# A mixer kernel whose last first-layer product is formed by seven block products for eight

## The chip, the cores and the metric

The kernel runs on one core of a Trainium2 chip. The metric is the device time of one execution in microseconds, as the median of several runs. TensorE (PE) multiplies matrices into PSUM, which has eight banks of 512 fp32 columns by 128 partitions; VectorE (DVE), ScalarE (ACT) and GpSimd (POOL) work element by element, the first two also on PSUM; SyncE (SP) issues nearly all transfers, in the order of its queue.

## What is computed

Attention with a few sink positions and a window, then a mixing of low rank along the sequence, then an FFN with a residual:

```python
B, H, S, D = 4, 8, 768, 64
scores = where(is_sink | in_window, q @ k.T / 8, -1e9)   # 4 sinks, window 128
a = softmax(scores) @ v                                  # per batch and head
x = a.transpose(0, 2, 1, 3).reshape(B, S, 512)
u = x + (x.T @ U @ V).T                                  # rank 32, along S
out = u + maximum(u @ w_ch1, 0) @ w_ch2                  # 512 -> 2048 -> 512
```

The inputs are 64-bit floats. The kernel narrows them to fp32, and keeps fp32 accuracy on PE by splitting an operand into a rounded high part and a rest, `hi + lo`: a product is then three matmuls, `hi*lo + lo*hi + hi*hi`.

## The kernel before

Lines are those of the kernel before. All work is written down as steps with an engine, a duration, what they read and write, and a rank (`Plan.add`, `Plan.any`, L232 on). `Plan.order` then plays the steps through with list scheduling: `forward` starts, in the order of time, the best-ranked step that is ready on each engine; `backward` derives new ranks from the latest times; eleven rounds run and the best planned end is kept. The steps are then issued in the order of their planned starts. So the order of every queue follows from the planned costs, `mm`, `dve`, `act`, `gps` (L420 on), and from the dependencies. Some steps may go to any of two or three engines (`copy` and `tt`), and the plan chooses. A buffer of a ring (`Ring`, `Box`) is waited for until the steps on its former content are done. PSUM banks are a free ring of eight.

**Batch 0 and batch 1** attend heads in pairs (`attend_pair`): scores of two heads (L652), then per block `soften`, a masked row minimum on DVE (L704) and an exponential with row sum on ACT (L707). `normalise` forms the inverse of the sums for each head (L715, reciprocal on DVE at L718) and scales. `transposes` turns the weights on PE (L745); for these batches the first part is masked by a product with a triangle on DVE as it leaves PSUM (L754), the second is copied and masked by a selection on POOL (L770). L675 multiplies by the values. **Batches 2 and 3** attend head by head (`attend`) with hi/lo operands (L695, L696, L793), and mask both parts on POOL (L767, L770). `mix_start`, `mix_half` and `mix_end` do the low-rank mixing (L889 to L982; L974 is its last product) and leave `uh` and `ul`, the transposed FFN input in high and low parts, by chunk of 384 rows.

**The FFN** (`ffn(b, c, ...)`) handles one chunk of 384 rows against 16 blocks of 128 features. `l1` is the first product of a block: 4 contraction slices x 3 matmuls of 384 columns (L1006, L1007, L1008) into one bank, then relu to `hh` on ACT or DVE (L1014, L1015) and the rest `hl` on DVE (L1017). `l2` is the second: for each of three row blocks three matmuls of 512 columns (L1027) into one of three banks held for the whole chunk. `l1(i)` is written ahead of `l2(i-1)`. For batch 0 the weights are narrowed on the way (`narrow`, L99 to L107, on DVE, ACT and POOL), and blocks other than 0 and 8 are stored as 1 MB units in `wd`, to be fetched again by the later batches through four tiles; blocks 0 and 8 stay resident in two more. At the end of a chunk DVE adds the residual (L1053) in `big` buffers, a ring of four which the narrowing of weights also uses, and SP stores the rows. L482 is where all of SP's transfers are issued.

Attention of batch b+1 is planned beside the FFN of batch b. Before the plan's first step there is a preamble with eight "spin" matmuls of zeros (L1320), the first loads, and the making of masks.

Of the kernel before, what the change touches and what calls it, by code (L numbers as in the profile page):

```python
# [9 lines left out]
F32 = mybir.dt.float32  # L10
# [11 lines left out]
P = 128  # L22
# [14 lines left out]
HALF = NBLK * SW  # L37
NEG = 8.0e9
# [3 lines left out]
NSPIN = 8  # L42
ROUNDS = 10
SLACK = 0.0344
SAME = 0.0842
PRICE = {"DVE": 3.0, "ACT": 1.5, "POOL": 1.5}
NBANK = 8
NRES = 2
# [14 lines left out]
LEAD = 30.0  # L63
BESIDE = ((6, 2.5), (0, 2.5), (0, 2.5))
# [10 lines left out]
def f32(ap):  # L75
    return ap.bitcast(F32)
# [163 lines left out]
class Plan:  # L240
# [35 lines left out]
    def order(self):  # L276
# [11 lines left out]
        for s, p in zip(self.steps, best[1]):  # L288
            s.prio = p
        self.forward()  # L290
        return sorted(self.steps, key=lambda s: (s.start, s.n))

    def backward(self):
# [20 lines left out]
        while done < len(self.steps):  # L314
# [5 lines left out]
            for p, whole in before[s]:  # L320
                p.left -= 1
                sync = self.SYNC[p.eng] if p.eng != e else (0.0 if e == "PE" else SAME)
                p.ready_b = max(p.ready_b, s.back + p.lat + sync + (1.95 if p.eng == "SP" else 0.0) if whole else s.back - p.dur)
# [6 lines left out]
    def forward(self):  # L330
# [37 lines left out]
        while done < len(self.steps):  # L368
            turn = sorted((max(avail[e], min(at(s, e) for s in lst)), e) for e, lst in ready.items() if lst)
            pick = None  # L370
# [19 lines left out]
            if e == "SP":  # L390
                dma = max(dma, t + s.dur + 0.65) + s.lat
                end = dma + 1.3
# [47 lines left out]
class Fast:  # L440
# [38 lines left out]
    def put(self, box, pair, nbytes, prio, r=(), part=None, rows=P):  # L479
# [3 lines left out]
        self.plan.add("SP", 0.5 if rows == P else 0.65, fn, r=r, w=((box, part),) if box else (), lat=nbytes / 330e3, prio=prio)  # L483

    def narrow(self, src, n, prio, dst=()):

        raw, A, S_ = self.raw(), self.nr(), self.nr()
        if len(self.early) > 0:
            self.early.pop(0)
        else:  # L490
# [143 lines left out]
    def attend_pair(self, b, pr, half, t0, qk, v, xT):  # L634
# [5 lines left out]
        sms = [self.ms(), self.ms()]  # L640
        for u in range(NBLK):
# [12 lines left out]
            add("PE", 0.105 + wd / 600.0, mms, r=[qr, kr] + [(p, u) for p in ps], w=sts, prio=t0, after=self.gate)  # L654
            for st, p, sm in zip(sts, ps, sms):
                self.soften(st, p, sm, u, lo, wd, qb, t0)
# [25 lines left out]
    def scores(self, half, t0, qs, kh, kl, qbase=0, kbase=0):  # L682
        nc, add = self.nc, self.plan.add
        p, sm = self.p(), self.ms()
        for u in range(NBLK):
# [12 lines left out]
            self.soften(st, p, sm, u, lo, wd, qb, t0)  # L698
        return p, sm

    def soften(self, st, p, sm, u, lo, wd, qb, t0):
# [4 lines left out]
            -0.125, 3.0e38, ALU.add, ALU.min, sm()[:, u:u + 1]), r=(st,), w=((p, u), (sm, u)), prio=t0)  # L706
        add("ACT", act(wd) + 0.22, lambda: nc.scalar.activation(  # L707
            p()[:, u, NS + lo:], p()[:, u, NS + lo:], AF.Exp, bias=sm()[:, u:u + 1], scale=-1.0,
# [694 lines left out]
```

## Time and profile before

| | us |
|---|---|
| median of 3 runs | 753.34 |
| lowest and highest | 753.15, 753.82 |
| span of the profiled execution, first to last instruction | 750.5 |

The profiled execution has a span only, which leaves out what lies around the instructions; the median is 2.84 us above it. The profile's page gives the busy time of each engine and how the span is spent, and the trace behind it can be asked for groups of instructions by line, for waits, for the chain of work that ended last, for a stretch in order of time, and for busy time by stage. Matmuls are pipelined: their durations overlap, and their spacing is read from their starts.

### The profile page before, as it was taken

The numbers are of one execution on the slowest core, as the hardware profiler recorded it, in microseconds if no ns is written. First come the engines' busy times: TensorE is split into PE (matmuls) and PEld (weight loads), VectorE is DVE, ScalarE is ACT, GpSimd is POOL, SyncE is SP. The second block draws the span as 40 slices with busy tenths as digits, with TensorE's granted clock in tenths as the row PEclk, the third lists the DMA queues.
The fourth block names the chain that finished last, engine by engine and source line by source line (L and its number), as shares of the span: only waits on it lengthen the run. The fifth ranks groups of instructions, "written<-read, shape, count | busy, mean of one in ns | idle before, by whom it ended". The sixth has DMA issues, their size and how long they took to land.

```text
span 750.5 us, 11587 instructions
## 1 busy us (share of the span) xinstructions
PE 727.3 (97%) x4012; PEld 629.2 (84%) x4012; DVE 454.3 (61%) x1168; ACT 341.4 (45%) x977; POOL 194.0 (26%) x316
## 2 busy tenths in 40 slices
PE   7989999999998999999999999999999999999997
PEld 5557777777787999999899899999999989889895
DVE  7999889798999577667751287675653131112111
ACT  6986475775874445555541164564441111111110
POOL 4652030421521263263510043544401000000000
PEclk9999999999999999999999999999999999999999
DMA  7466758755795378563575468760276536524752
GB/s 261 150 197 226 261 182 302 258 184 205 240 296 223 124 244 278 177 209 117 167 241 183 153 194 256 231 211 1 71 263 227 169 135 237 199 76 138 267 176 96
DMA packets 43780, 146.84 MB, mean 196 GB/s; under 512 B 5440, under 2 KB 12224, under 8 KB 34240
## 3 DMA queue, kind: packets, MB, share of 16 engines
q1 hardware_dynamic: 43424, 145.62, 57.7%
q8 instruction: 33, 0.54, 0.3%
q10 hardware_dynamic: 288, 0.39, 0.2%
q14 instruction: 35, 0.29, 0.1%
HBM read 116.37 MB, written 29.62 MB: 195 GB/s over the span
## 4 chain that ended last, share of the span: by engine, by line
PE 84%; DVE 11%; ACT 1%; issue 1%; DMA 1%; POOL 0%; SPq 0%; DVEq 0%; ACTq 0%
PE bank L1027 33%; PE bank L1006 12%; PE bank L1007 11%; PE bank L1008 11%; PE bank L793 3%; PE bank L745 2%; PE bank L652 2%; PE bank L675 2%; DVE nr L104 2%; PE bank L695 2%; PE bank L696 2%; DVE w L474 1%; DVE bank L106 1%; PE bank L906 1%; DVE p L704 1%
## 5 line engine op out<-in xcount | busy, mean ns | idle before, releaser
L1027 PE MATMUL bank<-w,hh 128*128 128x512 f32 x768 | 246.2, 402 | 1.2 <-ACT hh L1014 0.6
L1017 DVE SCALAR_TENSOR_TENSOR hl<-bank,hh 128x384 fp32r<-128x384 f32 x128 | 70.9, 554 | 186.9 <-ACT hh L1014 186.1
L1006 PE MATMUL bank<-ul,w 128*128 128x384 f32 x512 | 178.5, 349 | 0.8 <-ACT w L467 0.7
L1007 PE MATMUL bank<-uh,w 128*128 128x384 f32 x512 | 174.0, 340 | 1.8 <-DVE w L474 1.8
L1008 PE MATMUL bank<-uh,w 128*128 128x384 f32 x512 | 173.1, 338 | 0.0
L1014 ACT ACTIVATE hh<-bank 128x384 fp32r<-128x384 f32 x121 | 59.3, 490 | 236.6 <-PE bank L1008 235.9
L1027 PEld LDWEIGHTS bank<-w,hh 128*128 128x128 f32 x768 | 139.6, 189 | 24.5 <-issue 1.4
L1027 PE MATMUL bank<-w,hl 128*128 128x512 f32 x384 | 151.8, 395 | 2.3 <-DVE hl L1017 2.3
L1006 PEld LDWEIGHTS bank<-ul,w 128*128 128x128 f32 x512 | 96.3, 188 | 12.1 <-issue 3.4
L1007 PEld LDWEIGHTS bank<-uh,w 128*128 128x128 f32 x512 | 96.4, 188 | 8.6 <-DVE w L474 3.7
L1008 PEld LDWEIGHTS bank<-uh,w 128*128 128x128 f32 x512 | 96.2, 188 | 0.0
L1027 PEld LDWEIGHTS bank<-w,hl 128*128 128x128 f32 x384 | 72.2, 188 | 20.8 <-DVE hl L1017 3.6
L707 ACT ACTIVATE p<-p,ms 128x132 f32<-128x132 f32 (+1 forms) x144 | 69.9, 486 | 33.4 <-DVE ms L704 32.9
L704 DVE CUSTOM_DVE_ANT_0 p<-bank,mask 128x132 f32<-128x132 f32 (+1 forms) x144 | 54.3, 401 | 13.3 <-PE bank L696 10.8
L476 POOL TENSOR_TENSOR p<-p 128x256 f32<-128x256 f32 (+1 forms) x26 | 21.7, 836 | 131.0 <-ACT p L707 130.3
L476 POOL TENSOR_TENSOR ul<-xT,uh 128x384 fp32r<-128x384 f32 x14 | 14.4, 1050 | 146.0 <-ACT uh L467 146.0
L467 ACT COPY tb<-bank 64x384 f32<-64x384 f32 x31 | 14.7, 474 | 40.0 <-PE bank L793 40.0
L729 POOL TENSOR_TENSOR p<-p,r 128x396 f32<-128x396 f32 x27 | 24.2, 898 | 32.4 <-DVE r L718 26.0
L474 DVE TENSOR_TENSOR xT<-bank,tb 64x384 f32<-64x384 f32 x32 | 17.5, 548 | 23.1 <-ACT tb L467 22.8
L770 POOL TENSOR_SCALAR_AFFINE_SELECT oph<-oph 128x384 fp32r<-128x384 f32 (+1 forms) x48 | 27.4, 572 | 12.8 <-ACT oph L467 10.2
L745 PE MATMUL bank<-ident,p 128*128 128x128 f32 x144 | 24.9, 278 | 3.4 <-POOL p L729 2.2
L770 POOL TENSOR_SCALAR_AFFINE_SELECT opl<-opl 128x384 fp32r<-128x384 f32 (+1 forms) x48 | 26.1, 544 | 7.4 <-ACT opl L467 4.1
(187 smaller groups left out, 1137.7 us busy)
## 6 DMA issues: line engine op xcount, KB each, us to landing
w<-wd SPq DMA_DIRECT2D x60, 1024.0 KB, 4.9
big<-in_w_dram SPq DMA_DIRECT2D x32, 512.0 KB, 4.2
wd<-w SPq DMA_DIRECT2D x14, 1024.0 KB, 4.4
big<-xd SPq DMA_DIRECT2D x33, 256.0 KB, 3.2
qkraw<-in_k_dram SPq DMA_DIRECT2D x32, 198.0 KB, 5.3
qkraw<-in_q_dram SPq DMA_DIRECT2D x32, 192.0 KB, 4.0
out_dram<-big SPq DMA_DIRECT2D x24, 256.0 KB, 2.2
v_raw<-in_v_dram SPq DMA_DIRECT2D x16, 192.0 KB, 3.2
```

Of the source, the lines that this page charges most:

```text
L474: ways = {"DVE": (dve(n), lambda: nc.vector.tensor_tensor(dst(), a(), b(), op), pool)}
L476: ways["POOL"] = (gps(n), lambda: nc.gpsimd.tensor_tensor(dst(), a(), b(), op), True)
L704: add("DVE", dve(wd), lambda: nc.vector.tensor_tensor_reduce(p()[:, u, NS + lo:], st()[:, :wd], self.mask[:, min(qb, 2), lo:], -0.125, 3.0 ...
L707: add("ACT", act(wd) + 0.22, lambda: nc.scalar.activation(p()[:, u, NS + lo:], p()[:, u, NS + lo:], AF.Exp, bias=sm()[:, u:u + 1], scale=-1.0,
L745: nc.tensor.transpose(tr()[:, u * P:(u + 1) * P], p()[:, u, SW + NS:], self.ident)
L770: add("POOL", 0.126 + CH * 0.914e-3, lambda t=t: nc.gpsimd.affine_select(as_(t()[:, :, 1, :]), f32(t()[:, :, 1, :]), [[0, NBLK], [1, P]], ...
L1006: nc.tensor.matmul(ph()[:, :CH], wh, ul()[:, d, :], start=d == 0, stop=False)
L1007: nc.tensor.matmul(ph()[:, :CH], wl, uh()[:, d, :], start=False, stop=False)
L1008: nc.tensor.matmul(ph()[:, :CH], wh, uh()[:, d, :], start=False, stop=d == NC - 1)
L1014: self.plan.any({"ACT": (act(CH), lambda: nc.scalar.activation(hh(), ph()[:, :CH], AF.Relu)), "DVE": (dve(CH), lambda: nc.vector.tensor_sc ...
L1017: add("DVE", dve(CH), lambda: nc.vector.scalar_tensor_tensor(hl(), ph()[:, :CH], 0.0, f32(hh()), ALU.max, ALU.subtract), r=(ph, hh), w=(hl ...
L1027: nc.tensor.matmul(acc[k](), a()[:, sl], w()[:, m, :], start=not begin and i == 0 and j == 0, stop=i == n - 1 and j == 2)
```

## The change

1. **The last batch's FFN** is one pass over both chunks (`ffn_last`), by pairs of blocks. With the contraction in two halves, the features of a pair as two halves and the two chunks as two halves, a pair's first product is a 2x2 by 2x2 block product. It is formed by seven block products (Strassen's scheme, in the variant with shared sums) and not eight. Each product is 2 slices x 3 matmuls of 384 columns. Sums are gathered in two banks, x and y, with copies to SBUF between. The second product goes on as before, into six banks. `seven` prepares seven operands from batch 3's FFN input, in hi/lo parts, in buffers that attention has left; `sums` prepares four sums of the weight blocks of each pair, during the FFN of batch 1 (second chunk) and batch 2 (first chunk), and stores them as 1 MB units in `sd`. All 16 weight units are in `wd` now, and the six weight tiles are reused by pairs.
2. **Softmax inverses** of a pair of heads are formed by one reciprocal (`inverse`), and in batch 1 both masks are made on POOL (`late`).
3. **PE early:** 12 spin matmuls instead of 8, and 30 matmuls of zeros planned with the lowest rank.
4. **The planner** has other cost figures for matmuls, scores and transfers, knows when the first weights land (`EARLY`), and tries ranks shaken at random (three seeds), kept only where the planned end falls.
5. The kernel is built with a smaller scratch area for dynamic transfers.

```diff
+SUMS = {(1, 1): (0, 1, 2, 3), (2, 0): (7, 6, 5, 4)}
-NSPIN = 8
+NSPIN = 12
+NIDLE = 30
+SEEDS = (300012, 300023, 300026,)
+RATE = 360e3
+EARLY = (0.55, 1.5, 2.5, 3.8)
...
 def order(self):
+        for seed in SEEDS:
+            best = self.shaken(seed, best)
...
 def mm(n, k=1):
-    return k * max(n + (44 if n > CH else 34), 262) / 2400.0
+    return k * max(n * 1.085 + 6, 262) / 2400.0
...
 def put(...):
-        ... lat=nbytes / 330e3, prio=prio)
+        ... lat=nbytes / RATE, prio=prio)
...
 def attend_pair(...):
-        sms = [self.ms(), self.ms()]
+        sm = self.ms()
-            add("PE", 0.105 + wd / 600.0, mms, ...)
+            add("PE", 0.165 + wd / 600.0, mms, ...)
+        r = self.inverse(sm, 2 * NBLK, t0)
         for i in range(2):
-            self.normalise(b, 2 * pr + i, half, t0 + i, ps[i], sms[i], self.sinks[b])
-            ts += self.transposes(half, t0 + i, ps[i], True, self.opl if i else self.oph)
+            self.normalise(b, 2 * pr + i, half, t0 + i, ps[i], r, i * NBLK, self.sinks[b])
+            ts += self.transposes(half, t0 + i, ps[i], True, self.opl if i else self.oph, b > 0)
...
 def transposes(...):
-        if whole:
+        if whole and not late:
             ... product with the triangle on DVE ...
         else:
-            self.copy(CH, top, v3, psum=True, ...)
+            self.copy(CH, lambda: as_(top()), v3, psum=True, ...)
         for t in res:
-            if not whole:
+            if late:
                 add("POOL", 0.126 + nu * P * 0.914e-3, ... affine_select ...)
...
+    def seven(self, b, t0):
+        b11, b12, b21, b22 = src(0, 0), src(0, 1), src(1, 0), src(1, 1)
+        for i, x, y, ... in ((0, b12, b11, ...), (1, b22, t[0], ...), (2, b22, b12, ...), (3, b21, t[1], ...)):
+            for dd in range(2):
+                self.tt(CH, t[i](dd), x(dd), y(dd), ALU.subtract, ...)
+        for i, x, ... in ((0, b11), (1, b21), (2, b22), (3, t[3]), (4, t[0]), (5, t[1]), (6, t[2])):
+            for dd in range(2):
+                self.copy(CH, hi(dd), x(dd), ...)
+                self.tt(CH, lo(dd), x(dd), f32(hi(dd)), ALU.subtract, ...)
...
+    def sums(self, j, ws, prio):
+        for i, w in enumerate(ws):
+            self.tt(DM, fa()[:, i * DM:(i + 1) * DM], f32(w()[:, 0]), f32(w()[:, 1]), ALU.add, ...)
+        for i, o, x, y, op, r in ((0, s1, a21, a22, ALU.add, []), (1, s2, s1, a11, ALU.subtract, [(t, 0)]),
+                                  (2, s3, a11, a21, ALU.subtract, []), (3, s4, a12, s2, ALU.subtract, [(t, 1)])):
+            self.tt(K2, o, x, y, op, ...)
+        self.copy(2 * DM, hi, ft, ...)
+        self.tt(2 * DM, lo, ft, f32(hi()), ALU.subtract, ...)
+        for i, (x, y) in enumerate(((a, hi), (t, lo))):
+            self.put(sd, ..., 1 << 19, prio, r=(x,), part=i)
...
+    def ffn_last(self, b, prio):
+        order = late[2:] + [None] + late[:2] + [None]
+        def unit(key, dram):
+            i, old, f = slots.pop(0)
+            if f is None or f != key:
+                w = Box(lambda i=i: self.wtiles[i], (old,))
+                self.put(w, ..., 1 << 20, prio, r=(dram,))
+            slots.append((i, w, None))
+        def l1(n):
+            j = NPF - 1 - n
+            w1, w2, wt = unit(2 * j, self.wd[2 * j]), unit(2 * j + 1, self.wd[2 * j + 1]), unit(None, self.sd[j])
+            p1 = product(x, r12, w1, half(w1, 0), 0, True, self.line)
+            self.line = (p1,)
+            product(y, r2, w1, half(w1, 1), 1, True)
+            snap(sa, ta, 0)
+            plus(t11, tb, 1, sa, ta, 0)
+            relu(0, 0, t11, (tb, 1), False)
+            product(x, r12, wt, comb(1), 5)
+            product(y, r2, wt, comb(2), 6, True)
+            snap(sb, ta, 1)
+            product(x, r12, wt, comb(0), 4)
+            snap(sc, tb, 0)
+            plus(t22, tc, 1, sc, tb, 0)
+            relu(1, 1, t22, (tc, 1), False)
+            product(x, r12, wt, comb(3), 2)
+            relu(0, 1, r12, x, True)
+            product(y, r2, w2, half(w2, 1), 3)
+            plus(t21, tc, 0, sb, ta, 1)
+            relu(1, 0, t21, (tc, 0), False)
+        for n in range(NPF + 1):
+            if n < NPF:
+                l1(n)
+            if n == 0:
+                ... start six sums with vst and T ...
+            else:
+                l2(n - 1)
+        for k in range(NB):
+            o, ud = self.big(), self.xd[b][k]
+            ... load the residual, add on DVE, store ...
...
 def ffn(...):
+            if f // 2 in SUMS.get((b, c), ()) and f ^ 1 in fs[:i]:
+                self.sums(f // 2, pair, prio)
...
 def run(self):
+        for _ in range(NIDLE):
+            box = self.bank()
+            self.plan.add("PE", 0.22, lambda box=box: nc.tensor.matmul(box()[:, :P], zero, zero, ...),
+                          w=(box,), prio=1e6)
+            elif b == B - 1:
+                self.ffn_last(b, 70.0 + 80.0 * NCHUNK * b)
+                for f in range(NF) if b == 1 else ():
+                    if f not in STREAMED:
+                        self.put(self.wd[f], ..., 1 << 20, 200.0, r=(self.w[f],))
```

In this listing the arguments are shortened. `snap` is a copy from x, `plus` an addition of y to a copy, `relu` two operations.

## Rows read from the trace of the kernel before

**Rows 1.** The page, part 1: busy us, share of the span, instructions.
```profile
PE 727.3 (97%) x4012; PEld 629.2 (84%) x4012; DVE 454.3 (61%) x1168; ACT 341.4 (45%) x977; POOL 194.0 (26%) x316
```

**Rows 2.** Busy time by stage: stage and length, then engines, granted clock, DMA share, GB/s.
```profile
0.00:10.00 10.00, 7.70 (x40) 7.00 (x40) 5.45 (x32) 4.07 (x13) 2.39 (x14) 1.00 0.73 257
10.00:240.00 230.00, 215.23 (x1230) 163.57 (x1227) 213.15 (x577) 159.36 (x458) 74.15 (x105) 1.00 0.67 227
240.00:608.30 368.30, 367.77 (x2071) 335.85 (x2070) 212.95 (x523) 162.29 (x477) 117.48 (x197) 1.00 0.56 182
608.30:745.00 136.70, 136.62 (x678) 122.82 (x677) 22.07 (x40) 15.70 (x32) 0.00 (x0) 1.00 0.51 176
```

**Rows 3.** Order of time, 734 to 739 us, PE: start, duration, line, operation.
```profile
734.73 0.34 PE L1006 MATMUL bank<-ul,w 128*128 128x384 f32 x1
...
736.14 0.34 PE L1008 MATMUL bank<-uh,w 128*128 128x384 f32 x1
...
736.32 0.64 PE L1027 MATMUL bank<-w,hh 128*128 128x512 f32 x2
...
738.42 0.34 PE L1006 MATMUL bank<-ul,w 128*128 128x384 f32 x1
```

**Rows 4.** The chain that ended last, two neighbouring pieces: start, duration, what.
```profile
685.76 2.11 PE bank L1027 x9
689.99 2.11 PE bank L1027 x9
```

**Rows 5.** Order of time, same stretch, ACT and DVE; in brackets idle time before.
```profile
736.51 0.49 ACT L1014 ACTIVATE hh<-bank 128x384 fp32r<-128x384 f32 x1 [3.73 <-PE bank L1008]
...
737.04 0.56 DVE L1017 SCALAR_TENSOR_TENSOR hl<-bank,hh 128x384 fp32r<-128x384 f32 x1 [3.67 <-ACT hh L1014]
```

**Rows 6.** DMA issues: names, count, KB each, median us to landing; last the final additions.
```profile
w<-wd SPq DMA_DIRECT2D x60, 1024.0 KB, 4.9
...
big<-xd SPq DMA_DIRECT2D x33, 256.0 KB, 3.2
...
out_dram<-big SPq DMA_DIRECT2D x24, 256.0 KB, 2.2
```

**Rows 7.** Batch 3's last mixing product (order of time), and busy time by stage after.
```profile
564.29 0.34 PE L974 MATMUL bank<-vst,t 128*128 128x384 f32 x1
...
570.00:600.00 30.00, 30.00 (x151) 27.06 (x150) 3.90 (x7) 3.54 (x8) 0.00 (x0) 1.00 0.58 205
```

**Rows 8.** Groups by shape, DVE, 240 to 608.3 us: busy, mean ns, idle before.
```profile
L474 DVE TENSOR_TENSOR xhl<-first1q,xhl 128x512 fp32r<-128x512 f32 x5 | 3.5, 693 | 4.5 <-PE bank L929 4.0 <-ACT xhl L467 0.6
```

**Rows 9.** Order of time at 233 us.
```profile
228.21 4.04 DVE L982 TENSOR_TENSOR xT<-xT,bank 128x384 f32<-128x384 f32 x8
...
233.38 0.50 PE L1027 MATMUL bank<-w,hl 128*128 128x512 f32 x1 [2.11 <-DVE hl L1017]
```

**Rows 10.** Groups by shape, DVE, 0 to 240 us.
```profile
L718 DVE RECIPROCAL r<-r 128x3 f32<-128x3 f32 x32 | 4.5, 160 | 0.7 <-ACT r L715 0.7
L754 DVE TENSOR_TENSOR opl<-bank,tri 128x384 f32<-128x384 f32 x8 | 4.4, 550 | 0.5 <-ACT opl L467 0.4
...
L754 DVE TENSOR_TENSOR opl<-bank,tri 128x256 f32<-128x256 f32 x8 | 3.3, 416 | 0.2 <-PE bank L745 0.2
```

**Rows 11.** POOL's selections (f32: batches 0, 1), a DVE addition's mean, one addition at 15 us.
```profile
L770 POOL TENSOR_SCALAR_AFFINE_SELECT opl<-opl 128x384 fp32r<-128x384 f32 x32 | 16.6, 519 | 0.5
...
L770 POOL TENSOR_SCALAR_AFFINE_SELECT opl<-opl 128x384 f32<-128x384 f32 x16 | 9.5, 593 | 6.9 <-ACT opl L467 4.1 <-DVE opl L468 2.8
...
L474 DVE TENSOR_TENSOR p<-p 128x256 f32<-128x256 f32 x3 | 2.5, 826 | 0.0
...
15.53 0.39 DVE L474 TENSOR_TENSOR qkraw<-qkraw 128x256 f32<-128x256 f32 x1
```

**Rows 12.** Order of time, 6 to 13 us: three groups of score matmuls.
```profile
6.05 2.54 PE L652 MATMUL bank<-first0k,first0q 64*128 64x132 f32 x12 [1.45 <-DVE m_ck L161]
...
8.35 1.98 PE L652 MATMUL bank<-first1k,first1q 64*128 64x132 f32 x12
...
11.40 1.37 PE L652 MATMUL bank<-kh,qs 64*128 64x132 f32 x12 [1.06 <-DVE ms L704]
```

More of the change, by code (lines that the diff above doesn't have):

```diff
@@ L1 @@
+import random
 import struct
@@ L287, in order, with put_back, shaken @@
                 self.backward()
-        for s, p in zip(self.steps, best[1]):
-            s.prio = p
+        for seed in SEEDS:
+            best = self.shaken(seed, best)
+        self.put_back(best[1])
         self.forward()
         return sorted(self.steps, key=lambda s: (s.start, s.n))
+    def put_back(self, prios):
+        for s, p in zip(self.steps, prios):
+            s.prio = p
+    def shaken(self, seed, best):
+        rnd = random.Random(seed)
+        by, t, width = rnd.choice((0.3, 1.0, 3.0, 8.0)), rnd.uniform(-20.0, 260.0), rnd.choice((20.0, 60.0, 300.0))
+        if rnd.random() < 0.2:
+            t += 280.0
+        self.put_back(best[1])
+        self.forward()
+        for s in self.steps:
+            g = rnd.gauss(0.0, by)
+            if t <= s.start < t + width:
+                s.prio += g
+        for _ in range(TURNS):
+            try:
+                self.forward()
+            except ValueError:
+                break
+            if self.span < best[0] - 1e-6:
+                best = self.span, [s.prio for s in self.steps]
+            self.backward()
+        return best
     def backward(self):
@@ L322, in backward @@
                 sync = self.SYNC[p.eng] if p.eng != e else (0.0 if e == "PE" else SAME)
[L323 removed]
+                p.ready_b = max(p.ready_b, s.back + max(p.lat, 0.0) + sync + (1.95 if p.eng == "SP" else 0.0) if whole else s.back - p.dur)
                 if not p.left:
@@ L389, in forward @@
             end = t + s.dur + s.lat
-            if e == "SP":
+            if e == "SP" and s.lat < 0.0:
+                end = -s.lat
+                dma = max(dma, end - 1.3)
+            elif e == "SP":
                 dma = max(dma, t + s.dur + 0.65) + s.lat
@@ L482, in fn @@
             self.nc.sync.dma_start(d, s)
-        self.plan.add("SP", 0.5 if rows == P else 0.65, fn, r=r, w=((box, part),) if box else (), lat=nbytes / 330e3, prio=prio)
+        self.plan.add("SP", 0.5 if rows == P else 0.65, fn, r=r, w=((box, part),) if box else (), lat=nbytes / RATE, prio=prio)
     def narrow(self, src, n, prio, dst=()):
@@ L489, in narrow @@
             self.early.pop(0)
+            self.plan.add("SP", 0.0, lambda: None, w=(raw,), lat=-EARLY[NBIG - 1 - len(self.early)], prio=-1e6)
         else:
@@ L736, in normalise, with transposes @@
                       r=(p,), w=((psink, (half, h)),), prio=t0)
-    def transposes(self, half, t0, p, whole, own=None):
+    def transposes(self, half, t0, p, whole, own=None, late=True):
         nc, add = self.nc, self.plan.add
@@ L761, in transposes @@
         else:
-            self.copy(CH, top, v3, psum=True, r=(tr,), w=((res[0], 1),), prio=t0)
+            self.copy(CH, lambda: as_(top()), v3, psum=True, r=(tr,), w=((res[0], 1),), prio=t0)
+        if not whole:
             self.tt(CH, lambda: res[1]()[:, :, 1, :], v3, lambda: f32(top()), ALU.subtract, pool=False,
```

188 lines of the change are left out of this document (167 added, 21 removed).

## Prediction

> **What bounds the kernel now.** First the page's table of engines: TensorE (PE) is busy for 97% of the span [rows 1], so only a change to PE's work, or to what PE waits for, can move the end. Then busy time by stage [rows 2]. Three stages have to be told apart. From 240 to 608 us (FFN of batches 1 and 2, attention of 2 and 3 laid between) PE lacks 0.5 us of 368.3; from 608.3 to 745 us (FFN of batch 3) it lacks 0.1 us of 136.7, with VectorE (DVE) busy for 22 us and ScalarE (ACT) for 16. There a matmul taken away is time gained, and a microsecond taken from another engine is nothing. From 10 to 240 us PE lacks 14.8 us of 230 while DVE is busy for 213: DVE, which attends batches 0 and 1 and narrows the weights, sets the pace, and PE's idle time is what could be won. Since a busy PE need not be PE at its peak, 14.8 is a floor for that; 15 to 20 is my estimate. Before 10 us PE lacks 2.3 us.
>
> For PE's price I read starts, not durations: a matmul "lasts" 0.34 us, but from 734.73 to 736.14 us eight of the 384-wide ones start, 0.176 us each, and from 736.32 to 738.42 us nine of the 512-wide ones, 0.233 each [rows 3]. The chain of waits repeats every 4.23 us per feature block of `ffn` (689.99 less 685.76) [rows 4]: 12 of the first kind, 9 of the second. Nothing else fits in, and 2 x 16 x 4.23 = 135.4 us plus six starting matmuls is the whole stage.
>
> **The change, part by part.**
>
> (a) *Seven products for eight.* The first product of batch 3 has 2 chunks x 16 blocks x 12 = 384 matmuls of 384 columns. `ffn_last` has 8 pairs x 7 products x 6 = 336, as wide. Forty-eight fewer x 0.176 = **-8.45 us**, all in a stage without PE idle time. The second product keeps 288 matmuls of 512, and six start the sums in either. The new ideal of the stage is 8 x (42 x 0.176 + 36 x 0.2345) + 1.4 = 128.2 us instead of 136.7.
>
> (b) *Handoffs inside a pair.* Today a block's sum leaves PSUM once, and ACT (0.49 us) and DVE (0.56) do it beside 2.1 us of second-product matmuls [rows 5]. Now one bank, x, is read by a copy between product 4 and the product of `comb(3)`, with no other product between. Bare, that is 0.2 us until the copy starts (736.32 to 736.51), 0.49 for it and about 0.2 back: 0.9 us x 8 pairs = 7.2 us, an estimate from these rows. The other copies have a product of 1.06 us on bank y beside them. The cover is the second product of a neighbouring pair: 12 steps of 0.70 us, which the planner lays into any gap. Bounds 0 and 7.2; I take **+1.0**, near the covered end, because the like handoff of today costs PE nothing in 32 blocks of 32 [rows 2].
>
> (c) *Weights.* Six tiles of 1 MB now serve pairs of three (w1, w2, the sums), so pair n+2 loads into the tiles of pair n and cannot begin before its second product is read. A load takes 4.9 us from issue to landing [rows 6]. As the next pair's second product (8.4 us) can run meanwhile, and its first needs only w1 to begin, I cost it at nothing; without that cover it is a rival below. The bytes stay near 20 MB (12 blocks and 8 sums, where four blocks are still held), and the DMA engines are busy for 0.51 of the stage [rows 2].
>
> (d) *The tail.* Six blocks leave at the end instead of three, through four `big` buffers. Block 4's buffer waits for block 0: its add (0.69, as any 512-wide pass), output (2.2) and a load (3.2) [rows 6, 7], 6.1 us and some issue time, where the first block is done at most 5 x 1.41 = 7.0 us ahead of the last. Block 5 follows 1.4 us on. Bounds 0 (blocks 0 and 1 finished early) and +1.3; I take **+0.6**.
>
> (e) *Operands of the seven products.* `seven` replaces 8 copies and 8 subtractions by 14 copies and 22 subtractions. The last mixing matmul of batch 3 is at 564.3 us, 44 us ahead of its FFN, and DVE is busy for 3.9 us of the 30 from 570 [rows 8]. Fourteen more subtractions of 0.55 us are 7.7: covered, nothing. Without the cover, +7.7.
>
> (f) *Sums of weights.* `sums` makes, eight times, about ten 512-wide passes of at most 0.69 us [rows 7]: 55 us at most, over DVE, POOL and ACT, in two FFN chunks of batches 1 and 2. From 240 to 608 us DVE alone is idle for 155 us [rows 2]. It also issues 16 writes of 0.5 MB, and 2 of 1 MB go out for the resident blocks. All stand in SP's queue, in order, ahead of weight loads; a write whose subtraction is late holds those up. The price of a crowd is visible: at 233.4 us eight mixing additions stand before one `hl`, and PE waits 2.11 us [rows 9]. I take 0, and two such waits, +4, as the upper bound.
>
> (g) *Softmax inverses by pairs.* Batches 0 and 1 have 32 reciprocals by DVE, 4.5 us; half of them go, -2.3 us of DVE, since one of 6 elements should cost what one of 3 does [rows 10]. The second head's sums are now awaited by the first head too, about 0.5 us, inside a stage that DVE paces.
>
> (h) *Masks of batch 1.* Sixteen products with the triangle (eight of 0.55, eight of 0.416 us) leave DVE: -7.7 us [rows 10]. POOL gets 16 selections instead, of about 0.55: 8.8 us in a stage where it is busy for 74 of 230. So DVE loses 10.0 of its 213 us. What is that worth? At best all of it; at worst nothing, because PE's own idle time in the stage is but 15 to 20 us, and batch 1 is attended in the part of it where PE is idle least. About half, 5, is my figure; with 0.5 for (i) and 0.5 for a better order it makes 6.
>
> Whether the moved masks are free shows in POOL's rows: the same selection takes 593 ns in the early stage and 519 over the later batches, and a DVE addition of 128x256 with both inputs in SBUF took 0.39 us once and 826 ns on average [rows 11]. The two engines slow each other, by 13% for the selection. [...]
>
> (i) *PE kept busy early, and the planner.* [...] Four more spin matmuls and 30 idle ones, planned last in rank into gaps, could save up to some 1.8 us of PE in the two early groups, but DVE is the one awaited by then: -0.5. They can cost up to 0.2 us each where real work arrives behind one, 0 net at the low end. The new cost figures and three random reorderings can go either way; the reorderings are kept only where the planned end falls. I take -0.5 (0 to -4) for a better order. Early together: **-6.0**, bounds 0 and -12.
>
> Sum on the profiled span: 750.5 - 8.45 + 1.0 + 0.6 - 6.0 = 737.65. The median of the runs, 753.34, is 2.84 above that span; with it, **740.5 us**.
>
> **The rivals.**
>
> *Weights awaited (slower).* If the planner puts a pair's first product ahead of the previous pair's second, strictly, each load of (c) starts when the tile's last reader ends and PE has nothing left: six pairs x 4.9 us = 29 us, 770 us. It turns slower from the point where about 14 us, 2.3 per pair, is uncovered. For it: there are only six tiles. Against: the planner prices loads, and the steps are free to move. Chance 0.06.
>
> *The early stage gives nothing.* POOL and DVE share what the move was to free, and PE's own work limits the rest: 753.3 - 8.45 + 1.6 = 746.5 (745 to 749). Chance 0.18.
>
> *The early stage gives more than 10,* most of PE's 15 to 20 idle us, because DVE's relief and a better order come together: 734 (731 to 736). Chance 0.12.
>
> *Seven products, but eight's time.* The handoffs stay bare, 7.2 instead of 1.0: 746.7, and with no early gain 753, the same as before. So the change does not do what it says. Chance 0.04.
>
> **How the numbers follow.** My forecast, 740.5 (736 to 745), has 0.60. The range runs from 733 to 748: it holds the forecast, nearly all of the second rival, a part of the third, and the bounds of (b), (d) and (f) one at a time. A difference of 0.2%, 1.5 us, is about what a measurement of this kernel can tell from none. Faster by more: 0.60 + 0.18 + 0.12 and half of the last, 0.92. Within it: 0.02. Slower: 0.06.
>
> **What would show it.** In the changed kernel's stages: the last stage some 130 us long and PE waiting in it for 1 to 2 us, on ACT's copies of x; a wait on `w` there would be the first rival. The six output additions at the end bare or not show (d). PE still without waits from 240 us on shows (e) and (f). The FFN of batch 1 reached about 6 us sooner, with DVE less busy by some 10 us before it, shows (g) to (i); DVE relieved and the stage as long as before would show the second rival. The forecast is wrong if the last stage keeps its 136 us, or if PE starts to wait between 340 and 500 us.

## The result and the profile after

The changed kernel takes **746.66 us** (median of 6 runs, 744.72 to 747.85) where the kernel before takes 753.17 on the same chip: ratio **0.990**, 95% interval 0.988 to 0.992 (the two medians by themselves give 0.991). By the medians that is 6.5 us faster; the forecast was 12.8. The profiled spans are 745.7 and 750.5 us, 4.8 apart: the profiled execution of the kernel after took 747.4 us and is one of its longer ones, and that of the kernel before is, by its span, one of its shorter ones (later executions with that span took 752.3 us).

(For readers of the prediction: where it cites rows 7 it means what the list heads Rows 8, the 512-wide DVE pass, and where it cites rows 8, Rows 7, the stage from 570 us.)

Busy time by stage of the kernel after (start and end, length, then PE, PE's weight loads, DVE, ACT, POOL in us with instruction counts, granted clock, DMA share, GB/s), to be laid beside [rows 2]:

```profile
0.00:10.00 10.00, 8.28 (x54) 7.59 (x54) 6.34 (x37) 4.43 (x15) 2.89 (x15) 1.00 0.73 256
10.00:240.00 230.00, 221.58 (x1286) 173.37 (x1287) 205.61 (x539) 160.65 (x451) 81.13 (x120) 0.99 0.70 238
240.00:350.00 110.00, 110.00 (x641) 100.89 (x640) 75.40 (x198) 58.14 (x186) 41.85 (x77) 1.00 0.59 187
350.00:537.00 187.00, 182.40 (x1024) 162.87 (x1023) 135.02 (x306) 92.57 (x262) 79.36 (x110) 1.00 0.69 226
537.00:612.30 75.30, 75.30 (x400) 67.87 (x399) 35.87 (x71) 26.45 (x62) 14.55 (x18) 1.00 0.56 193
612.30:740.20 127.90, 127.90 (x634) 113.90 (x632) 35.83 (x64) 27.36 (x56) 0.00 (x0) 1.00 0.47 173
```

The last row is the Strassen stage, 128.0 us to the end of its last matmul at 740.3 us, PE without a gap. The fourth is new trouble: between the starts of the second FFN chunks of batches 1 and 2, where the sums of weights are made, PE lacks 4.6 us, and before it lacked 0.5 in 368 [rows 2]. In the second row DVE has 7.5 us less to do than before (over the first two together 6.7), and PE's 221.6 contain most of the idle matmuls.

The end of the stage, in order of time (start, duration, engine, line, operation, in brackets the idle time before):

```profile
739.46 0.86 PE L1209 MATMUL bank<-w,ul 128*128 128x512 f32 x3
740.36 0.69 DVE L1228 TENSOR_TENSOR big<-bank,big 128x512 f32<-128x512 f32 x1 [0.71 <-PE bank L1209]
```

DVE's last addition begins 0.04 us after the last matmul's modelled end: no buffer is awaited in the tail.

For stage lengths I use one mark per chunk, the start of the matmuls that add T (L1044 before, L1289 and L1220 after) to the chunk's sums, and for the last stage its first matmul:

| us | before | e5_shift | after |
|---|---|---|---|
| batch 1, first chunk | 261.1 | 260.5 | 259.5 |
| batch 1, second chunk | 352.2 | 351.3 | 350.4 |
| batch 2, second chunk | 531.4 | 529.5 | 536.7 |
| last stage begins | 608.1 | 605.6 | 612.3 |
| PE ends | 744.9 | 740.9 | 740.3 |

The middle column is the experiment that turned the account over; it comes first. Its stages that answer to the fourth and the last row above (same columns):

```profile
351.30:529.50 178.20, 177.60 (x1021) 162.34 (x1020) 105.54 (x263) 81.34 (x241) 60.69 (x102) 1.00 0.58 187
...
605.50:740.90 135.40, 135.38 (x679) 121.77 (x678) 22.25 (x39) 15.74 (x32) 0.00 (x0) 1.00 0.51 177
```

### The profile page after: what moved, and what is told of

It is laid out like the page before. It is cut to its first block, busy times and chain, and to the rows that moved or that the text cites. A ratio compares the mean times of both kernels' runs of the same rounds, so it can differ in the third digit from the quotient of the medians.

```text
span 745.7 us, 11814 instructions
## 1 busy us (share of the span) xinstructions
PE 725.6 (97%) x4032; PEld 626.5 (84%) x4032; DVE 494.8 (66%) x1209; ACT 369.6 (50%) x1029; POOL 219.8 (29%) x337
## 4 chain that ended last, share of the span: by engine, by line
PE 78%; DVE 9%; ACT 6%; DMA 4%; issue 2%; POOL 2%; SPq 0%; ACTq 0%; DVEq 0%; POOLq 0%
PE bank L1272 23%; PE bank L1209 9%; PE bank L1251 8%; PE bank L1139 8%; PE bank L1252 8%; PE bank L1253 7%; PE bank L693 2%; PE bank L840 2%; PE bank L791 2%; PE bank L717 2%; ACT p L749 1%; PE bank L737 1%; DMA qkraw<-in_q_dram 1%; PE bank L738 1%; DMA v_raw<-in_v_dram 1%
## 5 line engine op out<-in xcount | busy, mean ns | idle before, releaser
L1272 PE MATMUL bank<-w,hh 128*128 128x512 f32 x576 | 184.1, 401 | 0.0
L1251 PE MATMUL bank<-ul,w 128*128 128x384 f32 x384 | 134.2, 350 | 0.7 <-ACT w L507 0.5
L1252 PE MATMUL bank<-uh,w 128*128 128x384 f32 x384 | 129.3, 337 | 0.4 <-DVE w L514 0.3
L1253 PE MATMUL bank<-uh,w 128*128 128x384 f32 x384 | 129.2, 336 | 0.0
L1272 PEld LDWEIGHTS bank<-w,hh 128*128 128x128 f32 x576 | 103.6, 188 | 17.0 <-issue 2.4
L1272 PE MATMUL bank<-w,hl 128*128 128x512 f32 x288 | 114.2, 396 | 1.9 <-DVE hl L1262 1.9
L1259 ACT ACTIVATE hh<-bank 128x384 fp32r<-128x384 f32 x90 | 44.1, 490 | 92.7 <-PE bank L1253 92.2
L1251 PEld LDWEIGHTS bank<-ul,w 128*128 128x128 f32 x384 | 72.4, 188 | 9.4 <-issue 3.4
L1252 PEld LDWEIGHTS bank<-uh,w 128*128 128x128 f32 x384 | 72.3, 188 | 5.1 <-DVE w L514 1.4
L1253 PEld LDWEIGHTS bank<-uh,w 128*128 128x128 f32 x384 | 72.2, 188 | 0.0
L1272 PEld LDWEIGHTS bank<-w,hl 128*128 128x128 f32 x288 | 54.1, 188 | 15.5 <-DVE hl L1262 3.1
L1209 PE MATMUL bank<-w,ul 128*128 128x512 f32 x144 | 39.7, 394 | 0.0
L1209 PEld LDWEIGHTS bank<-w,ul 128*128 128x128 f32 x144 | 26.9, 187 | 6.0
```

Source lines behind the costliest of these rows:

```text
L1209: nc.tensor.matmul(accs[k](), a()[:, sl], w()[:, m, :], start=False, stop=n == NPF - 1 and f == 1 and q == 2)
L1251: nc.tensor.matmul(ph()[:, :CH], wh, ul()[:, d, :], start=d == 0, stop=False)
L1252: nc.tensor.matmul(ph()[:, :CH], wl, uh()[:, d, :], start=False, stop=False)
L1253: nc.tensor.matmul(ph()[:, :CH], wh, uh()[:, d, :], start=False, stop=d == NC - 1)
L1259: self.plan.any({"ACT": (act(CH), lambda: nc.scalar.activation(hh(), ph()[:, :CH], AF.Relu)), "DVE": (dve(CH), lambda: nc.vector.tensor_sc ...
L1272: nc.tensor.matmul(acc[k](), a()[:, sl], w()[:, m, :], start=not begin and i == 0 and j == 0, stop=i == n - 1 and j == 2)
```

## The experiments

Twelve kernels ran. Ratios are to the kernel before in the same session (753.0 to 753.3 us).

**e1 and e5: an address.** In the kernel after a feature block of `ffn` repeats every 4.18 us, before every 4.23 [rows 4], although neither `l1` nor `l2` was changed. Two side effects were at hand: the smaller scratch area for transfers, and, since the ring of row sums is twice as wide (`ms`, seven tiles of 32 bytes more), the place of every tile behind it. `uh` and `ul`, the moving operand, begin at a multiple of 64 bytes in their partition before, and 32 past one after.

```diff
 e1_scratch
-    nc = bacc.Bacc("TRN2", ..., num_devices=1)
+    nc = bacc.Bacc("TRN2", ..., num_devices=1, dynamic_dma_scratch_size=1024)
 e5_shift, in addition
-        sm = lambda: ms()[:, NBLK:]
+        sm = lambda: ms()[:, NBLK:2 * NBLK]
-        self.ms = ring(NSM, [P, 2 * NBLK], F32, "ms")
+        self.ms = ring(NSM, [P, 4 * NBLK], F32, "ms")
```

> The kernel before with the last part of the change alone, the smaller scratch area, so that only addresses in SBUF move. In the changed kernel's trace an FFN block takes 4.18 us where it took 4.23 before: its twelve 384-wide matmuls start 0.1735 us apart, not 0.176. Theory A, the addresses set this: 128 blocks x 0.047 = 6 us faster, 747 us, ratio 0.992, block 4.18 us. Rival B, the spacing belongs to the chip or the execution and not to the kernel: no change, ratio 1.000 within 0.002, block 4.23 us, or 4.18 without the kernel being faster than the kernel before on the same chip.

Measured: 753.04 us, ratio 1.0004 (0.9992 to 1.0016). The scratch area is worth nothing.

> The kernel before in its own order, nothing of the change in it; only the table of the softmax's row sums is twice as wide (and the DMA scratch is set as in e1_scratch), so that the moving operand of the FFN's products, uh and ul, begins 32 bytes past a multiple of 64 in its partition, as in the kernel after, and not at one, as before. Theory (the operand's place sets the spacing of the 384-wide matmuls): spacing 0.1735 us in place of 0.176 in the FFN's blocks of 24, so 4.18 us for a block in place of 4.23; 96 blocks x 0.05 = 4.6 us less, ratio about 0.994 (748.5 us where the kernel before takes 753.0). Rival (the spacing came with something else of the change): 4.23 us a block and a ratio of 1.000.

Measured: **749.38 us, ratio 0.995** (0.9932 to 0.9968). Neighbouring pieces of the chain of waits (start, duration, what), first of e5_shift, then of the kernel after:

```profile
686.52 2.10 PE bank L1027 x9
...
690.70 2.10 PE bank L1027 x9
```

```profile
404.70 2.10 PE bank L1272 x9
408.88 2.10 PE bank L1272 x9
```

Both are 4.18 us apart. So the kernel before, in its own order and with not one operation of the change, gains 3.8 us by the place of its tiles alone: more than half of the 6.5. On average over the last stage the 384-wide matmuls go from 0.1765 to 0.1736 us and the 512-wide ones from 0.2343 to 0.2330 (12 x 0.1736 + 9 x 0.2330 makes 4.18, 12 x 0.1765 + 9 x 0.2343 makes 4.23), so three quarters of it are in the 384-wide ones. The weight tiles lie ahead of `ms` and kept their place, so of what the 384-wide ones read only `uh` and `ul` moved; `hh` and `hl`, which the 512-wide ones read, moved as well. Whether the place of `uh` and `ul` is the cause, or that of another shifted tile in use at the time, was not told apart. From here on the change proper is what the kernel after does beyond e5_shift.

**e2 and e3: what the sums cost.** Both keep every instruction of the kernel after on PE in its order.

```diff
 e2_sd_small
-            self.put(sd, lambda i=i, y=y: (f32(sd()[:, 2 * i:2 * i + 2] ...), f32(y())), 1 << 19, ...
+            self.put(sd, lambda i=i, y=y: (f32(sd()[:, 2 * i, :64]), f32(y()[:, :64])), 1 << 19, ...
 e3_sums_thin
-            self.tt(DM, fa()[:, i * DM:(i + 1) * DM], f32(w()[:, 0]), f32(w()[:, 1]), ALU.add, ...)
+            self.tt(DM, fa()[:, i * DM:i * DM + 32], f32(w()[:, 0, :32]), f32(w()[:, 1, :32]), ALU.add, ...)
 ... and so for the other passes of sums; the writes keep their size
```

> The changed kernel in its own order, but the sixteen writes of weight sums carry 64 columns of 1024 each, and the last batch loads weight units of wd in their place, so that the result is not the reference's. All arithmetic stays. From 350 to 537 us the changed kernel loses 7 us against the kernel before. Theory A, the transfers do it (the DMA engines are busy for 1.0 of 370 to 400 and of 460 to 490): 6 to 7 us faster than the changed kernel, ratio 0.982, no stretch of that stage under 9.9 of 10 us of PE. Rival B, the arithmetic of the sums crowds DVE: 0 to 1 us faster, ratio 0.990.

> The changed kernel in its own order, but the arithmetic of the weight sums runs over 32 columns only, and the sixteen writes, still of 0.5 MB each, take their content from another tile, so that the result is not the reference's. Theory A, the transfers cost the 7 us between 350 and 537 us: 0 to 1 us faster than the changed kernel, ratio 0.990. Rival B, DVE's crowd does: 6 to 7 us faster, ratio 0.982, and DVE less busy by some 30 us.

Measured: e2_sd_small 742.2 us, ratio 0.9858 (0.9827 to 0.9888); e3_sums_thin 745.4, 0.9888 (0.9848 to 0.9927). From batch 1's second chunk to the last stage it takes 261.9 us after, 258.0 in e2, 258.2 in e3, and 254.3 in e5_shift, which has no sums. So each half removed gives back some 3.8 of the 7.6 us by which the kernel after is longer there, and in the profile neither theory held alone. In the medians of the runs e2 is 4.5 us below the kernel after, between its two theories, and e3 1.3, near that of the transfers. PE's idle time in the same piece is 4.6 us after, 3.95 without the arithmetic and 2.1 without the writes; it leaves out waits that are shorter than a matmul's modelled duration, so it doesn't divide the loss. The larger parts of the two pieces, e2 first, to be laid beside the fourth row of the kernel after:

```profile
349.30:530.90 181.60, 179.90 (x1019) 162.31 (x1019) 133.09 (x303) 92.53 (x261) 79.73 (x109) 1.00 0.58 188
...
351.40:534.20 182.80, 178.85 (x1021) 162.24 (x1020) 111.31 (x303) 87.56 (x261) 59.93 (x109) 1.00 0.70 230
```

These are single executions, and they scatter: e4 below issues the same matmuls in this piece as the kernel after, with all of the sums, and takes 259.8 us. By the timed runs e2 is clearer than e3, whose interval covers that of the kernel after: that the writes cost some 4 us is shown, the 3.7 of the arithmetic rests on the profile. Ten-microsecond stretches of the kernel after, and the same of e2_sd_small (columns as above):

```profile
370.00:380.00 10.00, 9.54 (x60) 8.42 (x60) 9.53 (x18) 4.11 (x7) 3.13 (x3) 1.00 1.03 342
380.00:390.00 10.00, 9.10 (x47) 7.71 (x46) 5.83 (x10) 4.38 (x9) 1.29 (x1) 1.00 0.97 330
390.00:400.00 10.00, 10.00 (x52) 9.11 (x51) 8.60 (x17) 5.67 (x11) 2.99 (x3) 1.00 1.01 352
...
470.00:480.00 10.00, 9.34 (x57) 8.06 (x58) 9.29 (x26) 7.58 (x27) 6.12 (x11) 1.00 1.02 359
```

```profile
370.00:380.00 10.00, 9.54 (x61) 8.33 (x60) 9.38 (x18) 5.71 (x11) 2.61 (x3) 1.00 0.70 231
380.00:390.00 10.00, 10.00 (x50) 8.83 (x50) 6.95 (x12) 4.65 (x8) 0.30 (x1) 1.00 0.95 299
390.00:400.00 10.00, 10.00 (x54) 9.20 (x52) 7.57 (x15) 4.00 (x8) 2.99 (x3) 1.00 0.85 307
...
470.00:480.00 10.00, 10.00 (x64) 9.20 (x65) 9.14 (x26) 8.36 (x28) 9.52 (x14) 1.00 0.91 254
```

In these stretches of the kernel after the DMA engines are busy all the time (share 1.0) and carry 330 to 359 GB/s; in e5_shift no such stretch between 350 and 540 us is above 0.94. Where blocks follow each other without attention between, a block needs 1 MB of weights each 4.2 us, some 250 GB/s, and a pair's sums add 1 MB of writes per 8.4 us, 125 more. That is 375, an estimate from the block's time: about the most that was seen in such stretches, first in e3_sums_thin, then in e4:

```profile
390.00:400.00 10.00, 10.00 (x52) 9.11 (x52) 6.58 (x14) 4.78 (x11) 2.97 (x3) 1.00 1.02 377
...
460.00:470.00 10.00, 9.05 (x47) 7.28 (x45) 8.52 (x22) 7.03 (x24) 5.22 (x5) 1.00 1.02 379
```

DVE is crowded too: it is busy for 9.5 us of the ten from 370 us, in e5_shift for 5.3. DMA issues (names, count, KB each, median us to landing) of the kernel after:

```profile
w<-wd SPq DMA_DIRECT2D x52, 1024.0 KB, 5.4
...
sd<-big SPq DMA_DIRECT2D x16, 512.0 KB, 7.2
```

A half-megabyte write takes 7.2 us to land and stands in one queue with the loads for the next attention. The chain of waits of the kernel after names those loads (start, us, what):

```profile
457.24 8.03 DMA v_raw<-in_v_dram
...
504.05 9.14 DMA qkraw<-in_q_dram
```

Queries and values of the next batch arrive late (over the whole kernel such loads take 4.6 us each in the median; before, 4.0 and 3.2), and then the attention steps that would fill PE come late. Whether the two halves add up to the whole loss against e5_shift is not settled: no kernel leaves out both, the order differs too, and e11 below shows what that can do.

**e4: the idle matmuls.** The order is planned as in the kernel after, but the 30 matmuls of zeros aren't issued, and the spin matmuls are 8 again and not 12.

```diff
-NSPIN = 12
+NSPIN = 8
-            self.plan.add("PE", 0.22, lambda box=box: nc.tensor.matmul(box()[:, :P], zero, zero, ...),
+            self.plan.add("PE", 0.22, lambda box=box: box() and None,
```

> The changed kernel in its own order without its 30 planned idle matmuls and with 8 spin matmuls. In the changed kernel PE's granted clock falls to 0.5 from 11.7 to 14.4 us and from 52.6 to 55.4 us, which the kernel before does not show. Theory, the idle matmuls bring nothing, since DVE and transfers pace the stage: within 1 us of the changed kernel, ratio 0.990 within 0.002. Rival, they hold the clock up or fill it: without them the clock falls more often, and the FFN of batch 1 begins 1 to 3 us later, ratio 0.993.

Measured: **743.1 us, ratio 0.9864** (0.9844 to 0.9884), some 3 us better than with them, which neither the theory nor the rival had. The 30 and the 4 were not told apart. The idle ones hold PE for 8.3 us between 10 and 45 us, in two halves each (a group of PE's table there: count, busy us, mean ns, idle before):

```profile
L1376 PE MATMUL bank<-const-float32-0.0 128*128 128x128 f32 x54 | 8.3, 294 | 0.0
```

and they stand where the plan saw a gap, which is not always where the chip has one: PE still waits 1.93 us at 9.5 and 1.10 at 49 us.

**e6 and e7: the parts alone.** Both in the layout of e5_shift. e6 has only the inverses by pairs and batch 1's masks on POOL; e7 only the Strassen product with its sums.

```diff
 e6_pairs_masks (to the kernel before)
-        sms = [self.ms(), self.ms()]
+        sm = self.ms()
+        r = self.inverse(sm, 2 * NBLK, t0)
-        if whole:
+        if whole and not late:
 ...
 e7_strassen_alone (to the kernel after)
-NSPIN = 12
-NIDLE = 30
-SEEDS = (300012, 300023, 300026,)
-RATE = 360e3
+NSPIN = 8
+NIDLE = 0
+SEEDS = ()
+RATE = 330e3
 ... costs, EARLY, inverse and masks as before
```

> The kernel before with the softmax inverses by pairs and batch 1's masks left to GpSimd, in the shifted layout of e5_shift; no Strassen products, no idle matmuls, no changed costs. Theory A (the trace of after: VectorE's relief before the first FFN is worth little): 0 to -1.5 us beyond e5_shift, the first FFN of batch 1 at most 1.5 us sooner than in e5_shift. Theory B (my prediction's sum: this relief is worth about 5 us): -5 us beyond e5_shift, the first FFN 5 us sooner.

> The kernel after with only the Strassen product of the last batch, its sums and its weight units; inverses by head, masks, start, costs and order of loads as before; shifted layout. Theory A (what the traces show: last stage -8.9 us, stage of the sums +7, shifted layout -4.5): about -6 us against before, ratio 0.992, that is about -2 us beyond e5_shift. Theory B (the sums are paid only because the changed costs and order drew the work together): the stage of the sums loses under 2 us and the kernel is some 12 us under before, ratio 0.984.

Measured: e6_pairs_masks **755.85 us, 1.0031** (1.0013 to 1.0050); e7_strassen_alone **756.02, 1.0030** (1.0007 to 1.0052). Both are 6.5 us over e5_shift; no theory had that. The trace shows PE's clock. One-microsecond stretches of e6_pairs_masks:

```profile
47.00:48.00 1.00, 0.87 (x11) 0.43 (x6) 1.00 (x3) 1.00 (x5) 0.90 (x1) 1.00 0.97 287
48.00:49.00 1.00, 0.00 (x0) 0.00 (x0) 1.00 (x3) 0.60 (x4) 0.62 (x3) 1.00 0.67 257
49.00:50.00 1.00, 0.00 (x0) 0.00 (x0) 1.00 (x4) 0.72 (x4) 0.83 (x1) 0.97 0.97 368
50.00:51.00 1.00, 0.89 (x4) 0.56 (x4) 1.00 (x4) 1.00 (x5) 0.00 (x0) 0.50 0.63 212
...
55.00:56.00 1.00, 1.00 (x6) 1.00 (x6) 0.97 (x2) 0.66 (x2) 0.00 (x0) 0.50 0.70 74
56.00:57.00 1.00, 1.00 (x8) 1.00 (x7) 0.97 (x3) 0.34 (x2) 0.00 (x0) 0.62 0.61 197
```

PE waits 2.24 us for ACT's scaling of softmax weights (47.9 to 50.1), and when it has work again the granted clock is 0.50 until 56.6 us. Summing (1 - granted clock) over the span's five-microsecond stretches, such falls take 6.8 us of PE's full speed in e6_pairs_masks, 8.5 in e7, 3.4 in the kernel after, 1.7 in e4, and none in the profiles of before and e5_shift. Each fall in the profiles comes at the end of a pause of PE or shortly behind one, and the pauses are 0.5 to 3.7 us long, in e7 3.27 in one case. But pauses as long are also seen without a fall: 2.11 us at 231 us before [rows 9], 2.50 at 379 us in e3, 2.91 at 213 us in e10. Nor is the kernel before free of falls in other executions: in the same session its mean granted clock ran from 0.998 down to 0.989, and its time from 752.3 to 757.6 us. Over ten timed executions each, the median clock was 0.988 in e6, 0.989 in e7 and 0.9945 in e5_shift, so lower clocks go with the longer times in these runs too. How much of the 6.5 us the falls are, and how much the new orders, was not told apart. In e6 the clock rises again after 6.5 us of work, and the fall that the kernel after has near 53 us is missing from the profiles of e2 and e3, which issue the same instructions on PE.

**e8: the sums spread out.** e4 with the sums in other chunks.

```diff
-SUMS = {(1, 1): (0, 1, 2, 3), (2, 0): (7, 6, 5, 4)}
+SUMS = {(1, 1): (4, 5, 6, 7), (2, 1): (0, 1, 2, 3)}
```

> e4_no_idle (after without the 30 idle matmuls) with the sums of the weights spread wider: four of eight units in the second FFN chunk of batch 1 and four in the second of batch 2, none in the first chunk of batch 2. Theory (the sums cost because a chunk that writes four units needs 1 MB of fetches and 1 MB of writes at the rate the queues can just carry; two such chunks with a quiet one between them let the fetches catch up): the loss between the start of batch 1's second chunk and of the last batch falls from about 5 to 3 us, time 741 where e4_no_idle took 743.1. Rival (each unit costs its transfer wherever it stands): 743 again.

Measured: 744.1 us, 0.9862 (0.9827 to 0.9897), the rival's 743 within its spread. The second chunk of batch 2 then takes 90.3 us to the next mark in place of e4's 81.3, and the one before it 92.2 in place of 99.2: as far as one newly planned order can tell, the sums cost what they cost wherever they stand. (Falls of the clock, one at 550 us, take 5.1 us of PE's speed in this profile.)

**e9 to e12: orders with shorter gaps.** If the falls were the cost, an order without long gaps should free the parts' worth. The planner's measure of an order now charges for gaps; the planner then shakes ranks with 20 seeds or so, found by that measure.

```diff
+    def cost(self):
+        end, cost = 0.0, self.span
+        for s in sorted((s for s in self.steps if s.eng == "PE"), key=lambda s: (s.start, s.n)):
+            cost += min(2.0, max(0.0, 2.0 * (s.start - end - 0.9)))
+            end = max(end, s.start + s.dur)
+        return cost
-            if self.span < best[0] - 1e-6:
+            if self.cost() < best[0] - 1e-6:
```

> e6_pairs_masks (inverses by pairs, batch 1's masks to GpSimd, no Strassen product, no idle matmuls) with another order of the same steps: the planner shakes its priorities as in the kernel after, and its score charges 2 us for each microsecond (2 at most) of an idle gap of PE beyond 0.9 us. Planned span 715.64 us; e6's was 722.37, before's 723.85. Theory A (e6 lost its 6.5 us against e5_shift to the halved clock after PE's gaps at 20.5, 48 and 230 us): with the gaps shorter, falls of the clock cost under 2 us, and the time goes with the planned span, 8 us under e5_shift's 749.4: 741 to 743. Theory B (moving work from VectorE to GpSimd and ScalarE costs in itself): 752 or more.

> e7_strassen_alone (Strassen product and sums, nothing of the early stage's edits) with its order shaken and scored in the same way. Planned span 710.98 us where e7's was 718.08. Theory A (e7's 756 us were falls of the clock after PE's gaps at 41, 58 and 235 us, some 8.5 us, and the sums, some 5): 756 - 8 - 7 = 741. Theory B (the Strassen product's own traffic and arithmetic make it dearer than the trace of after tells): 748 or more.

> The kernel before in the shifted layout of e5_shift with nothing but its order shaken and scored in the same way; no part of the change otherwise. Planned span 718.92 us where before's is 723.85. Theory A (the order by itself is worth what the plan says, and is part of what the change gained): 749.4 - 4.9 = 744.5, up to 747 if the planned gap of 2.1 us at 37 us brings a fall of the clock. Theory B (a reshuffled order is worth nothing on the chip, as e6 and e7 suggest): 749 to 752.

> e8_quiet (the whole change without its 30 idle matmuls, sums in the second chunks of batches 1 and 2) with its order shaken further and scored in the same way, the idle matmuls' places not counted as work. Planned span 713.89 us where e8's was 715.66; the longest planned gap of PE before 200 us is 1 us. Theory A (falls of the clock cost e8 some 5 us): 744.1 - 4 - 1.8 = 738 to 740. Theory B: 743 to 745 as e8 and e4.

Measured: e9 751.99 (0.9975, 0.9957 to 0.9993), e10 750.51 (0.9957, 0.9942 to 0.9972), e11 **755.83** (1.0030, 1.0015 to 1.0045), e12 746.61 (0.9912, 0.9886 to 0.9937). Half of theory A stood: the mean granted clock rose from 0.989 to 0.999 and from 0.987 to 0.996, and e9 and e10 are 3.9 and 5.5 us under e6 and e7. The other half fell: e9 and e10 came out where theory B had them, e11 and e12 above both theories, and none came near its planned time. The planner's own figure beside the profiled span:

| kernel | planned | span | difference |
|---|---|---|---|
| e5_shift | 723.85 | 746.5 | 22.7 |
| e11, its order shaken | 718.92 | 754.2 | 35.3 |
| e6 | 722.37 | 752.3 | 29.9 |
| e9, shaken | 715.64 | 749.1 | 33.5 |
| e7 | 718.08 | 753.5 | 35.4 |
| e10, shaken | 710.98 | 749.1 | 38.1 |
| after (other costs) | 715.01 | 745.7 | 30.7 |
| e4 (other costs) | 715.01 | 741.4 | 26.4 |
| e12 (other costs), shaken | 713.89 | 744.9 | 31.0 |

e11 is the plainest: the same operations as e5_shift in another order that the plan holds to be 4.9 us shorter take 7.7 us more. Its PE is idle for 3.5 us more (span less busy time, 26.9 against 23.4), and falls at 15 to 25 and 50 to 55 us take 3.4. So any edit here that makes the planner plan again brings a shift of up to some 8 us of its own, and the early parts can't be priced from e6 to e12. Only kernels that keep an order (e1, e5, e2, e3, e4) price anything more closely, and a stage read from one profile of each to some 2 us, as e4 against the kernel after shows.

## Why the prediction was partly right

The range held the time, the sign was right, and the forecast was 6.2 us too low. By its own terms, against e5_shift, on the profiled spans, which are single executions (by these the change beyond e5_shift is worth 0.9 us, by the medians of the runs 2.7). The 2.84 us that the prediction put between span and median hold 1.7 that lie between the two in one execution (745.7 and 747.4 of the kernel after); the rest is that the profiled execution before was a short one.

- **(a), (b) and (d), the last stage: right.** Forecast -8.45 + 1.0 + 0.6 = -6.85. Measured from the stage's first matmul to the end of the span, 141.0 to 133.4, **-7.6**, of which 7.3 lie ahead of PE's last matmul. The handoffs cost nothing that shows (PE busy for 127.90 of 127.90, and its matmuls start nearly as closely as in e5_shift), so the cover by the neighbouring pair's second product held to the end of its bounds, and the tail is bare of waits. Against the kernel before itself the stage's matmuls take 8.8 us less, 1.5 of it by the address. (The ideal stage of (a) adds up to 128.1, not 128.2.)
- **(c), weights: right** at nothing, in the kernel after. The rival of weights awaited did not occur; in e12, in another order, one such load (7.42 us in its chain at 651 us) leaves PE idle for 0.5 us, and the stage is 0.7 us longer.
- **(e): not told apart** from (f); no wait after 537 us, where `seven` runs, so nothing is charged to it.
- **(f), the sums: the step that failed.** Forecast 0, at most +4; measured **+7.7** from batch 1's first chunk to the last stage (345.1 to 352.8), and +5.5 in e4 with the same matmuls there. In the order of the kernel after the writes account for 3.9 of it (e2, with the runs) and the arithmetic for 3.7 (e3, one profile); how much of the 7.7 belongs to the new order itself is open, for e9 and e11, which have no sums, take 349.0 and 348.8 us for the same piece in their orders. The step counted DVE's idle time over 368 us, and of the transfers only their places in SP's queue. It never set the rate of the stage itself, fetches and writes together, against what the queues carry; 0.56 as a mean share [rows 2] hid stretches in which a chunk with sums takes all of it, and DVE's 155 idle us hid that DVE is full in the same stretches. The prediction did name the sign to look for, PE starting to wait between 340 and 500 us, and that is where 3.4 of its 4.6 idle us lie; the rest is at 516 us.
- **(g) to (i), early: mis-sized.** Forecast -6.0, measured **-0.9** at batch 1's first FFN. DVE's relief came nearly as worked out: 7.5 us less in the stage, where (g) and (h) made 10.0. Sixteen reciprocals of six take 183 ns and not the 160 of those of three [rows 10], so (g) is -1.6, not -2.3; groups of the kernel after, 0 to 240 us, first DVE's, then POOL's (busy us, mean ns, idle before):

```profile
L760 DVE RECIPROCAL r<-r 128x6 f32<-128x6 f32 x16 | 2.9, 183 | 0.0
```

```profile
L817 POOL TENSOR_SCALAR_AFFINE_SELECT opl<-opl 128x384 f32<-128x384 f32 x16 | 9.7, 605 | 1.1 <-ACT psink L780 0.6 <-ACT opl L507 0.3
```

  What went wrong is that (i) costs: the falls of the clock (3.4 us of PE's speed in this profile), which were not foreseen, and the idle matmuls themselves, whose cost the prediction named and took as 0 net. That the 1.8 us behind the term of -0.5 can be gained no run shows: after twelve spin matmuls the first two groups of [rows 12] do take 1.37 and 1.52 us, but the third, behind a wait of 1.93 us and with the granted clock at 0.50 from 12 to 14 us, takes 2.54 and starts no sooner (11.42 us). Without the idle matmuls e4 reaches that FFN 3.0 us before e5_shift, and e2, whose profile has no early fall, 2.1. How much (g) and (h) are worth by themselves stays open; e9, at a mean clock of 0.999, reaches it 1.2 us sooner with 5.3 us less of DVE.
- **POOL beside DVE.** That the two share what the move of the masks was to free, as the second rival has it, no run shows: DVE's busy time did fall by 7.5 us, and the selection of `opl` takes 605 ns where it took 593 [rows 11], that of `oph` 581 where it took 587. The 593 and 519 ns from which the prediction read a slowing of 13% are selections with different output types as well as of different stages, so they do not show that by themselves.
- **Outside the sum: -4.0** by the address.

So -7.6 - 0.9 + 7.7 - 4.0 = -4.8, as the spans have it. The rival "the early stage gives nothing" named 746.5, which is nearly the measured time, but not for its reason: it left out an unmeant gain of 4 and a loss of 7.7 that in part cancel. That the range held the time is luck in the same way: without the unmeant 4 us it would have been near 750.5, outside.

The best of these kernels are e4 and e8, the change without its idle matmuls: 0.986 of the time before, with intervals of 0.984 to 0.988 and 0.983 to 0.990, against 0.988 to 0.992 for the change as it was made.

## What to carry to other kernels

Where a stage streams weights, add the new bytes, and the new passes, to what the stage does in the very stretches where they fall, and compare the sum with what queues and engines are seen to carry; a mean share over a long stage doesn't tell. Before giving a change the credit, run the old kernel with only the change's side effects (buffer sizes, so addresses): here that was more than half of the gain. And where a planner orders everything anew, test parts in kernels that hold the order, or count a fresh order as several microseconds of noise.

## What was unexpected of the hardware

- The mean spacing of 384-wide fp32 matmuls went from 0.1765 to 0.1736 us, and that of 512-wide ones from 0.2343 to 0.2330, when the tiles behind one ring, among them the moving operand of the former, moved by 32 bytes modulo 64 in their partition.
- Some pauses of PE of about 0.5 to 3.7 us were followed by stretches of 3.4 to 10.2 us at a granted clock of 0.50, after the work had come back; each took 1.7 to 5.1 us of PE's full speed. Other pauses, of up to 2.9 us, were not, and whether a fall occurs differed between executions of the same instructions.
- Writes of 0.5 MB beside a stream of fetches took 7.2 us to land, and the 1 MB fetches went from 4.9 to 5.4 us (medians over the whole kernel).
